# Output rows 12 to 15 of an attention kernel: other order of their products, other place in a step

## The chip, the cores and the metric

The kernel runs on one core of one Trainium2 chip. The metric is the time of one execution on the device in microseconds (us); the median of three runs is 1478.57 us (1478.53 to 1479.0).

## What is computed

Two attention branches over the same input x (2048 positions, width 512, 32 heads of 16) are mixed by a gate. Cut to what matters:

```python
g = sigmoid((x * gate_w).sum(-1, keepdims=True))
# branch A: each position sees itself and 7 earlier ones, 2 apart
a = attention_A(x @ wqkv) @ A_wo
# branch B: full attention, 32 query heads over one head of keys and values
q, k, v = x @ wq, x @ wk, x @ wv
b = softmax(q k^T / 4) v @ B_wo
return g * a + (1 - g) * b
```

All in float32. The kernel multiplies in a reduced format and wins the accuracy back by splitting a factor into a high and a low part, so that one product becomes three: high by high, high by low, low by high.

## The kernel before, in words

Branch B is the long part. It is cut into 32 units (`NU`; 8 groups of heads by 4 blocks of 512 queries) of 16 steps (128 keys each), 512 steps (`NS`) in one loop at the end of the kernel. A step s does, on TensorE (PE):

- the scores, in two pairs of matmuls (`exp_pair`, L487), one pair for each of the banks `eb[0]` and `eb[1]`; ScalarE (ACT) takes the exponential of each pair (L489, 1024 elements a partition) as soon as it stands;
- the weighted sum of the step before, eight matmul instructions into the bank `po` (`weighted`, L497);
- where there are any left, matmuls for the maxima that a later unit will need: a pair into `m2` (`pm` in the profile, L330) between the two pairs of scores, and a single one into `m1` (`ps`) behind them. VectorE (DVE) reduces them (L357, L368). They run ahead of the steps; the last ones, for unit 31, are done in step 480.

At the end of a unit DVE transposes `po` (L511), and some small work on DVE and GpSimd (POOL) makes half a chunk of branch B's output for its 512 positions (`finish_a`, `finish_b`, `finish_c`; then the unit is in `shaped`). Unit 29 is the last one that the last rows wait for before their final chunk: its steps end with step 479.

The output has 16 rows of 128 positions. A row is a sum of products of 512 columns: 12 for branch A (index k = 0: four chunks in three parts, from the tiles `turned`) and, in the last four rows, 9 for branch B (k = 1: three chunks, from the tiles `own`); the fourth chunk comes after the last step. Each product is two matmuls of 64 rows (L848), both halves of the array at once. Rows 12 to 15 are made by the generator `spread`, one product per `yield 0.0`, all into the bank `m2`, which the maxima no longer need then. `spread_some(k)` draws up to k products from it; the loop calls it once a step. What a row needs:

- `blocks_out(j)`, L692: DVE transposes the row of branch A in blocks (L696) into `raw`; `blocks_in` sends that to memory (L701) and back in another order with 16 small DMAs (L707), all on the queue of SyncE (SP);
- `parts_a(j)`, L823: POOL splits it into the two `turned` tiles (two copies L828, two subtractions L831);
- `prepare(j)`, L655: POOL splits branch B's chunks into the two `own` tiles (L660, L665);
- at the end of a row, a copy and an addition on DVE (L867, L868) take the sum out of `m2`; the next row's first product writes `m2` again.

Each of `turned` and `own` has one buffer, so the next row's parts are written when the present row has read the old ones.

The order of instructions on every engine is fixed when the program is built. A small planner keeps a clock per engine (`clk`), gives operations estimated durations (`T_R`, `T_EXP`, ...) and decides by them in which step something is put. `tasks` holds work with a due time, and `run_tasks` at the end of a step issues what is due. The number of products of a step comes from `row_prods` (84 at first): so many are given that 10 (`TO_END`) are left when the steps are over, and at most 4. They run beside the last chain on DVE, from the last weighted sum to the output.

Unit 31's maxima, made in steps up to 480, go back as two extra rows of its queries (`shift_d`, L475): four small DMAs on SP and four on POOL. They must be there when step 496 begins.

Of the kernel before, what the change touches and what calls it, by code (L numbers as in the profile page):

```python
# [19 lines left out]
C = D // P  # L20
# [4 lines left out]
NU = NQB * NHG  # L25
# [12 lines left out]
NS = NU * NJ  # L38
# [3 lines left out]
TO_END = 10  # L42
# [7 lines left out]
def gated_mix_kernel(ctx, tc, xt, wa, wk, wq, wo_a, wo_b, out):  # L50
    nc = tc.nc
# [26 lines left out]
    m2 = pp.tile([P, 2, 512], F32, name="pm")  # L78
# [7 lines left out]
    clk = {"pe": 0.0, "act": 0.0, "dve": 0.0}  # L86
# [221 lines left out]
    half = []  # L308
    free = {"m2": 0.0, "m1": 0.0, "e0": 0.0, "e1": 0.0, "po": 0.0}
    tasks, shifted, pm = [], set(), []  # L310
    hooks, pool, done = [], 0.0, set()
# [20 lines left out]
    def to_go():  # L332
        return 2 * len(slots) + len(half)
# [148 lines left out]
    def exp_pair(s, pr, other=False, first=0):  # L482
        bank, key = (m2, "m2") if other else (eb[pr], f"e{pr}")
        u, kt = divmod(s, NJ)
        for odd in (first, 1 - first):
            b = 64 * odd
            nc.tensor.matmul(bank[:, odd, :], kst[b:b + 64, kt * P:(kt + 1) * P], qst[home(u)[0]][b:b + 64, pr, :], start=True, stop=True)  # L487
        e = px.tile([P, 2, 512], F32, name="pexp", bufs=6)
        nc.scalar.activation(e, bank, AF.Exp, scale=SCALE)  # L489
        free[key] = after("act", after("pe", free[key], T_R) + T_LAT, T_EXP)  # L490
        exped[s] = free[key]
        pexp[s, pr] = e
# [162 lines left out]
    def prepare(j, n, copy=None):  # L655
        nonlocal pool
        hi, lo = turned[j, 1] = [pe[0].tile([P, C, P], F32R, name=f"own{x}", bufs=1) for x in range(2)]
        own = ob[j // 4][:, :n, j % 4 * P:(j % 4 + 1) * P]
        if copy:
            copy(hi[:, :n], own)  # L660
            at = max(clk["pe"], pool / 1e3) + 1.3
        else:
            nc.scalar.activation(hi[:, :n], own, AF.Copy)
            at = after("act", clk["pe"], 0.6)
        nc.gpsimd.tensor_sub(lo[:, :n], own, hi[:, :n].bitcast(F32))  # L665
        pool = max(pool, 1e3 * at) + 1300
# [25 lines left out]
    def blocks_out(j):  # L692

        own = p2[0].tile([P, D], F32, name="raw", bufs=1)
        for k in range(2):
            nc.vector.transpose(own[:, k * D // 2:(k + 1) * D // 2], oa[k][:, j, :])  # L696
        after("dve", 0, 0.9)
        tasks.append((clk["dve"] + 0.3, blocks_in, (j, own)))
# [7 lines left out]
                    dst = oa[k][32 * m:32 * m + 32, j, c * P:(c + 1) * P].rearrange("p (a z) -> p a z", a=4)  # L706
                    nc.sync.dma_start(dst, v[m][:, 2 * k + c])  # L707

    def out_items(j, n):
        items = []  # L710
        for k, m in ((1, n), (0, C)):
            for x, w in ((0, woh), (0, wol), (1, woh)):
                items += [(lambda c=c, x=x, k=k: turned[j, k][x][:, c, :], w[k][:, c, :]) for c in range(m)]
        return items
# [104 lines left out]
    def spread(js, n):  # L819

        m = 3 * (C + n)

        def parts_a(j):  # L823
            nonlocal pool
            hi, lo = turned[j, 0] = [pe[0].tile([P, C, P], F32R, name=f"turned{x}", bufs=1) for x in range(2)]
            for k in range(2):
                own = oa[k][:, j, :].rearrange("p (c q) -> p c q", c=2)
                nc.gpsimd.tensor_copy(hi[:, 2 * k:2 * k + 2], own)  # L828
            for k in range(2):
                own = oa[k][:, j, :].rearrange("p (c q) -> p c q", c=2)  # L830
                nc.gpsimd.tensor_sub(lo[:, 2 * k:2 * k + 2], own, hi[:, 2 * k:2 * k + 2].bitcast(F32))  # L831
            pool = max(pool, 1e3 * clk["pe"]) + 2600

        prepare(js[0], n, nc.gpsimd.tensor_copy)
        yield 1.0
        parts_a(js[0])
        yield 1.0
        while slots or half:
            yield 1.0
        for j in js:  # L840
            nxt = j + 1 if j != js[-1] else None
            items = []
            for i in range(m):
                items = items or out_items(j, n)
                st, mv = items[i]
                for b in range(2):
                    h = slice(64 * b, 64 * b + 64)
                    nc.tensor.matmul(m2[:, b, :], st()[h], mv[h], start=(i == 0), stop=(i == m - 1 and (b == 1 or nxt is not None)))  # L848
                after("pe", 0, T_R)
                row_prods[0] -= 1  # L850
                row_left[0] = m - 1 - i
                if i == 1 and nxt:
                    blocks_out(nxt)
                if i == 3 * n and nxt:
                    prepare(nxt, n, nc.gpsimd.tensor_copy)
                if i < m - 1:
                    yield 0.0
            del turned[j, 0], turned[j, 1]
            x = len(parts)
            if x < 2:  # L860
                spare.append(p2[0].tile([P, 512], F32, name="part", tag=("own", "tr8")[x], bufs=1))
            elif x == 2:
                two = p2[0].tile([P, 2, 512], F32, name="part", tag="pr", bufs=1)
                spare.extend([two[:, 0, :], two[:, 1, :]])
            parts[j] = spare[x]
            if nxt:
                nc.vector.tensor_copy(parts[j], m2[:, 1, :])  # L867
                nc.vector.tensor_add(parts[j], m2[:, 0, :], parts[j])  # L868
                parts_a(nxt)
                after("dve", clk["pe"] + T_LAT, 1.4)  # L870
                yield 1.5
        done.add("last")

    def spread_some(k):

        while (k > 0 or row_left[0] == 1) and later_rows and spread_at[0] <= clk["pe"]:
            x = next(later_rows[0], None)
            if x is None:
                later_rows.clear()
            else:  # L880
                spread_at[0] = clk["pe"] + x
                k -= 1
# [190 lines left out]
    last = len(lumps) - 1  # L1073
# [69 lines left out]
    for s in range(NS + 1):  # L1143
        u, kt = divmod(s, NJ)
        if s == 16 * NB + 4:
            half_back()
        if len(stacked) < NU and s > 16 * (home(len(stacked))[1] + 1):
            stack(len(stacked))
        if s < NS and kt == 0 and u not in shifted:
            while u not in shifted:  # L1150
                clk["pe"] += 0.5
                run_tasks()
                if u not in shifted and left.get(u, 1):
                    assert pause(4)
        v = min(x[0][0] for x in (half, slots, [(NU,)]) if x)
        need = left.get(v, NF // NU)
        steps = 16 * v - 6 - s
        short = need - 2.8 * max(0, steps) if v < NU else 0
        lead = (NF - to_go()) / 64 - s / 16
        order = (0, "m2", "later") if s else ()  # L1160
        rows = 4 if outs else 8
        k, n = (outs + rows) // 4 - 1, C - (outs >= NJ - 4)
        if outs == NJ - 4:
            if s == 16 * NU - 40:
                blocks_out(outs)
            if NU - 3 in shaped and to_go() <= 9 and not later_rows and "last" not in done:
                later_rows.append(spread(list(range(outs, NJ)), n))
            if short > 0 and steps < 2:
                pause(short)
        elif due or outs < NJ and s and kt == 0 and outs // NH in done and NHG * (k + 1) - 1 in shaped and (lead < LEAD or s >= 16 * (NHG * (k + 2) + 1)):  # L1170
            if not due:
                prepare(outs, n)
                due.append(n)
            else:
                out_phase(list(range(outs, outs + rows)), due.pop(), kt == 1)
                outs += rows
                order = (0, "m1", 2)
        elif short > 0 and steps < 2:
            pause(short)

        first = 0
        order = list(order)
        while order:
            which = order.pop(0)
            if which == "later":
                order = ["m1", 1] if free["e1"] > clk["pe"] - E1S else [1, "m1"]
                first = 0
            elif which == "m2":
                fill_ready("m2", M2S)
            elif which == "m1":  # L1190
                if not later_rows and (kt or not s or u >= NU - 8) and singles(s):
                    first = half[0][4] if half else 0
                    fill_ready("m1", M1S)
            elif s < NS:
                exp_pair(s, which % 2 or which // 2, which == 2, first)
        spread_some(min(4, -(-(row_prods[0] - TO_END) // (NS + 1 - s))))
        if s:
            weighted(s - 1)
            if kt == 0 and s < NS:
                finish_a(u - 1, nc.gpsimd)  # L1200
        run_tasks()
        run_pool()
# [63 lines left out]
```

## Time and profile before

| what | value |
|---|---|
| median of three runs | 1478.57 us |
| the profiled execution's own time | 1480.36 us |
| its span in the profile | 1478.3 us |
| PE busy | 1463.2 us, 99% of the span |
| ACT busy | 1274.7 us, 86% |
| DVE busy | 1193.8 us, 81% |
| POOL busy | 1034.4 us, 70% |

The profile is one execution. In it L12 is line 12 of the kernel, `pe`, `pm`, `ps`, `po` are the banks `eb`, `m2`, `m1`, `po`; PEld is the loading of weights, SPq the queue on which SP issues DMAs. A row of the timeline gives start, duration, engine, line, operation, output and inputs, and how many instructions were merged; in brackets stands the idle time before it and who ended that. The chain of waits is the work that ended last, followed back from the end: start, duration, engine, tile, line.

### The profile page before, as it was taken

Reading aid. Unit: us, or ns where it says so; the run is one execution under the profiler, and the core shown is the slowest. Engines: PE = TensorE matmul, PEld = TensorE weight load, DVE = VectorE, ACT = ScalarE, POOL = GpSimd, SP = SyncE. Lnnn points to the kernel's source line nnn. Section 1 sums busy time; section 2 is a strip of 40 time slices with the busy share of each in tenths; the row PEclk is TensorE's granted clock in tenths of the full one; section 3 lists DMA queues with packets and bytes.
Section 4 is the critical chain, followed back from the end, with each engine's and each line's share of the span. In section 5 each row is a group of like instructions: output and inputs, shape, how many; then the busy total and the mean of one; then the engine's idle time right before and its main releaser. Section 6 shows DMA issues by size and latency. Waiting matters only on the chain.

```text
span 1478.3 us, 29547 instructions
## 1 busy us (share of the span) xinstructions
PE 1463.2 (99%) x10996; PEld 708.2 (48%) x10996; DVE 1193.8 (81%) x1855; ACT 1274.7 (86%) x1646; POOL 1034.4 (70%) x1828
## 2 busy tenths in 40 slices
PE   9999999999999999999999999999999999999998
PEld 5998989533333333333333376333333363333343
DVE  6976667789888898888888888889888878888612
ACT  5468988999999999999999978999999988999985
POOL 7876988887988979888889898888888330011221
PEclk9999999999999999999999999999999999999999
DMA  6754323121220211202102011121120000000111
GB/s 223 209 150 136 92 85 122 34 84 42 66 76 10 85 59 41 71 12 70 51 32 81 31 64 67 42 70 42 41 71 12 12 26 16 12 1 2 25 28 36
DMA packets 54080, 89.86 MB, mean 61 GB/s; under 512 B 18800, under 2 KB 35232, under 8 KB 49712
## 3 DMA queue, kind: packets, MB, share of 16 engines
q1 hardware_dynamic: 46928, 48.99, 11.4%
q0 software_dynamic: 6432, 37.94, 7.8%
q8 instruction: 86, 1.41, 0.4%
q10 hardware_dynamic: 576, 1.05, 0.2%
q14 instruction: 58, 0.48, 0.1%
HBM read 60.07 MB, written 27.35 MB: 59 GB/s over the span
## 4 chain that ended last, share of the span: by engine, by line
PE 90%; ACT 3%; POOL 3%; DMA 1%; issue 1%; DVE 1%; DVEq 0%; ACTq 0%; POOLq 0%
PE po L497 34%; PE pe L487 23%; PE pm L330 8%; PE ps L330 7%; PE pe L1094 6%; PE pe L783 4%; PE pm L422 2%; PE ps L422 1%; PE pm L848 1%; POOL qlo L222 1%; ACT dd L432 1%; DMA ad<-stage 1%; POOL qraw L215 1%; PE po L422 1%; PE pe L185 1%
## 5 line engine op out<-in xcount | busy, mean ns | idle before, releaser
L489 ACT ACTIVATE pexp<-pe 128x1024 f32<-128x1024 f32 x1022 | 989.5, 1022 | 95.9 <-PE pe L487 94.1
L357 DVE TENSOR_REDUCE mx<-pm 128x2 f32<-128x1024 f32 x495 | 605.7, 1224 | 118.6 <-PE pm L330 114.8
L497 PE MATMUL po<-pexp,vst 128*32 128x512 f32 x4096 | 545.5, 605 | 0.0
L487 PE MATMUL pe<-qst,kst 64*128 64x512 f32 x1916 | 431.9, 448 | 1.2 <-ACT pexp L489 1.2
L487 PEld LDWEIGHTS pe<-qst,kst 64*128 64x128 f32 x1916 | 179.2, 183 | 476.5 <-ACT pexp L489 470.8
L368 DVE TENSOR_REDUCE mx<-ps 128x1 f32<-128x512 f32 x481 | 327.1, 680 | 3.7 <-PE pe L487 1.9
L330 PE MATMUL pm<-kst,qst 62*128 62x512 f32 x945 | 192.2, 396 | 0.3 <-DVE mx L357 0.3
L561 POOL TENSOR_TENSOR pr<-aext 128x256 f32<-128x256 f32 x256 | 183.1, 742 | 4.3 <-ACT dd L432 4.1
L330 PE MATMUL ps<-kst,qst 62*128 62x512 f32 x455 | 180.1, 396 | 0.2 <-DVE mx L442 0.2
L621 POOL TENSOR_TENSOR oa<-oa,av 128x256 f32<-128x256 f32 x224 | 164.3, 734 | 15.2
L497 PEld LDWEIGHTS po<-pexp,vst 128*32 128x32 f32 x4096 | 80.5, 108 | 178.1 <-issue 169.1
L618 POOL TENSOR_TENSOR av<-aext,lg 128x256 f32<-128x256 f32 x224 | 139.6, 623 | 12.7
L1094 PE MATMUL pe<-wah,xh 64*128 64x384 f32 (+1 forms) x504 | 109.3, 338 | 0.4 <-ACT gate L255 0.4
L1094 PE MATMUL pe<-wal,xh 64*128 64x384 f32 (+1 forms) x504 | 109.7, 338 | 0.0
L1094 PE MATMUL pe<-wah,xl 64*128 64x384 f32 (+1 forms) x504 | 109.5, 337 | 0.0
L432 ACT ACTIVATE dd<-pm 128x512 f32<-128x512 f32 x164 | 90.9, 607 | 17.6 <-PE pm L422 11.9
L442 DVE CUSTOM_DVE_ANT_0 dd<-ps,dd 128x512 f32<-128x512 f32 x82 | 56.7, 692 | 56.7 <-PE ps L422 29.6
L524 POOL TENSOR_TENSOR rl<-rl,gate_t 128x16 f32<-128x16 f32 x31 | 6.9, 222 | 126.2 <-DVE rl L518 125.7
L330 PEld LDWEIGHTS pm<-kst,qst 62*128 62x128 f32 x945 | 91.9, 187 | 2.8 <-DVE mx L357 1.2
L330 PEld LDWEIGHTS ps<-kst,qst 62*128 62x128 f32 x455 | 84.8, 186 | 5.6 <-DVE mx L368 1.7
L567 POOL TENSOR_TENSOR tr<-pr 128x512 f32<-128x512 f32 x64 | 81.8, 1278 | 4.1
L567 POOL TENSOR_TENSOR tr<-tr 128x256 f32<-128x256 f32 (+1 forms) x128 | 72.5, 567 | 8.3
(215 smaller groups left out, 1893.8 us busy)
## 6 DMA issues: line engine op xcount, KB each, us to landing
aext<-ad POOLq DMA_DIRECT2D x32, 1056.0 KB, 5.5
ad<-stage SPq DMA_DIRECT2D x32, 384.0 KB
qst<-qd SPq DMA_DIRECT2D x60, 128.0 KB
xraw<-xt SPq DMA_DIRECT2D x16, 256.0 KB
qd<-qhi SPq DMA_DIRECT2D x16, 256.0 KB
qd<-qlo SPq DMA_DIRECT2D x16, 256.0 KB
qst<-qd SPq DMA_DIRECT2D x60, 64.0 KB
qst<-ml SPq DMA_DIRECT2D x216, 2.0 KB
```

Source lines behind the costliest of these rows:

```text
L330: nc.tensor.matmul(dst, qst[home(v)[0]][b:b + 62, pr, t * P:(t + 1) * P], kst[b:b + 62, kc * 512:(kc + 1) * 512], start=True, stop=True)
L357: nc.vector.tensor_reduce(m[:, :, pr, t, kc], dst, AX.X, ALU.max)
L368: nc.vector.tensor_reduce(m[:, odd, pr, t, kc:kc + 1], dst, AX.X, ALU.max)
L432: nc.scalar.activation(dd[0][:, odd], m2[:, odd, :], AF.Abs)
L487: nc.tensor.matmul(bank[:, odd, :], kst[b:b + 64, kt * P:(kt + 1) * P], qst[home(u)[0]][b:b + 64, pr, :], start=True, stop=True)
L489: nc.scalar.activation(e, bank, AF.Exp, scale=SCALE)
L497: nc.tensor.matmul(po[32 * i:32 * i + 32, :], vst[:, kt, :], pexp[s, i // 2][:, i % 2, :], start=(kt == 0), stop=(kt == NJ - 1))
L561: nc.gpsimd.tensor_mul(pr[:, k], q, e[:, o:o + NH, AC:2 * AC])
L567: nc.gpsimd.tensor_add(nx, cur[:, :, 0:n], cur[:, :, n:2 * n])
L618: nc.gpsimd.tensor_mul(av, e[:, o:o + NH, 2 * AC:].rearrange("p j (h d) -> p j h d", d=DH), lg[:, w].unsqueeze(3).to_broadcast([P, NH, AG, ...
L621: nc.gpsimd.tensor_add(ao, ao, av)
L1094: nc.tensor.matmul(front[2 if x == last else x % 2][0][:, b, :n], l[h], r[h], start=(i == 0), stop=(i == 3 * C - 1))
```

## The change

It does four things to rows 12 to 15:

1. Within a row the 12 products of branch A come first and branch B's 9 after them. So `parts_a` of the next row is issued after the 12th product, and `prepare` of the next row at the row's end; before it was the other way round.
2. The generator is created without waiting for unit 29 to be shaped. It issues `parts_a(12)` first, then waits until no maxima are left and until `m2` is free by the planner's clock. `prepare(12)` is issued as soon as unit 29 is shaped; only the 10th product of row 12 waits for that.
3. `blocks_out` runs a row further ahead: rows 12 and 13 in steps 472 and 480 (before: row 12 in step 472 alone), and the others two rows ahead.
4. The products of a step are given out between its first and its second pair of scores, no longer behind both.

```diff
-    def out_items(j, n):
+    def out_items(j, n, ks=(1, 0)):
         items = []
-        for k, m in ((1, n), (0, C)):
+        for k, m in [(k, n if k else C) for k in ks]:
...
-        prepare(js[0], n, nc.gpsimd.tensor_copy)
-        yield 1.0
         parts_a(js[0])
         yield 1.0
-        while slots or half:
+        while slots or half or free["m2"] > clk["pe"] + 0.1:
             yield 1.0
         for j in js:
             nxt = j + 1 if j != js[-1] else None
             items = []
             for i in range(m):
-                items = items or out_items(j, n)
+                if j == js[0] and i < 3 * C and (j, 1) not in turned:
+                    while i == 3 * C - 3 and NU - 3 not in shaped:
+                        yield 1.0
+                    if NU - 3 in shaped:
+                        prepare(j, n, nc.gpsimd.tensor_copy)
+                items = items or out_items(j, n, (0, 1))
...
-                if i == 1 and nxt:
-                    blocks_out(nxt)
-                if i == 3 * n and nxt:
-                    prepare(nxt, n, nc.gpsimd.tensor_copy)
+                if i == 1 and j + 2 <= js[-1]:
+                    blocks_out(j + 2)
+                if i == 3 * C and nxt:
+                    parts_a(nxt)
                 if i < m - 1:
                     yield 0.0
             del turned[j, 0], turned[j, 1]
+            if nxt:
+                prepare(nxt, n, nc.gpsimd.tensor_copy)
...
                 nc.vector.tensor_add(parts[j], m2[:, 0, :], parts[j])
-                parts_a(nxt)
...
-            if s == 16 * NU - 40:
-                blocks_out(outs)
-            if NU - 3 in shaped and to_go() <= 9 and not later_rows and "last" not in done:
+            if s in (16 * NU - 40, 16 * NU - 32):
+                blocks_out(outs + (s - 16 * NU + 40) // 8)
+            if to_go() <= 9 and not later_rows and "last" not in done:
...
+        some = min(4, -(-(row_prods[0] - TO_END) // (NS + 1 - s)))
...
             elif s < NS:
+                if which == 1:
+                    spread_some(some)
                 exp_pair(s, which % 2 or which // 2, which == 2, first)
-        spread_some(min(4, -(-(row_prods[0] - TO_END) // (NS + 1 - s))))
+        if s == NS:
+            spread_some(some)
```

## The prediction

> **What bounds the kernel now.** I read the page first, then the chain of waits, then the timeline of the last hundred microseconds, engine by engine.
>
> ```profile
> PE 90%; ACT 3%; POOL 3%; DMA 1%; issue 1%; DVE 1%; DVEq 0%; ACTq 0%; POOLq 0%
> ```
>
> PE carries 90% of the chain that ended last. Before step 477 PE is full (scores, maxima and weighted sums), and the change does not touch that part. So only the last 32 steps count. They look like this in the chain of waits:
>
> ```profile
> 1387.50 0.43 PE pe L487 x2
> 1387.93 0.23 PE pm L330 x2
> 1388.17 0.25 PE pe L487 x2
> 1388.41 1.00 PE po L497 x8
> ...
> 1392.07 1.95 ACT pexp L489 x2
> 1394.02 0.04 issue
> 1394.06 0.50 PE pe L487 x2
> ...
> 1406.18 0.66 PE pe L487 x4
> 1406.84 0.70 PE pm L848 x6
> 1407.54 1.00 PE po L497 x8
> ...
> 1465.35 0.42 PE pm L848 x2
> ```
>
> Three kinds of step stand there. While maxima are left, PE does first scores, a pair for the maxima, second scores, weighted sum: 0.43 + 0.23 + 0.25 + 1.00 = 1.91 us of work. When the maxima are over (step 481 on) the chain goes through ACT: the second scores at 1394.06 start only when two exponentials have ended. From 1406 on the chain is PE alone: 0.66 + 0.70 + 1.00 = 2.36 us for a step with three products, so a product costs 0.70 / 3 = 0.23 us and a bare step 2.36 - 0.70 = 1.66 us.
>
> I number the steps back from the last scores, step 511, and measure a step from its first scores on PE to the next step's:
>
> ```profile
> 1393.36 0.49 PE L487 MATMUL pe<-qst,kst 64*128 64x512 f32 x2
> ...
> 1403.52 0.96 PE L487 MATMUL pe<-qst,kst 64*128 64x512 f32 x4
> 1406.11 0.73 PE L487 MATMUL pe<-qst,kst 64*128 64x512 f32 x4
> ...
> 1420.25 0.75 PE L487 MATMUL pe<-qst,kst 64*128 64x512 f32 x4
> 1422.82 0.73 PE L487 MATMUL pe<-qst,kst 64*128 64x512 f32 x4
> 1423.42 1.94 ACT L489 ACTIVATE pexp<-pe 128x1024 f32<-128x1024 f32 x2 [0.63 <-PE pe L487]
> ...
> 1458.18 0.51 PE L487 MATMUL pe<-qst,kst 64*128 64x512 f32 x2
> 1458.91 0.50 PE L487 MATMUL pe<-qst,kst 64*128 64x512 f32 x2 [0.23 <-ACT pexp L489]
> 1460.80 0.74 PE L487 MATMUL pe<-qst,kst 64*128 64x512 f32 x4
> 1462.93 0.96 PE L487 MATMUL pe<-qst,kst 64*128 64x512 f32 x4
> 1463.53 1.94 ACT L489 ACTIVATE pexp<-pe 128x1024 f32<-128x1024 f32 x2 [0.19 <-PE pe L487]
> 1465.70 1.07 PE L497 MATMUL po<-pexp,vst 128*32 128x512 f32 x8
> ```
>
> Step 481 begins at 1393.36, step 486, the first with products, at 1403.52, step 511, the last, at 1462.93. Steps 481 to 485 take 10.16 us, 2.03 each, of which PE works 1.66. That is the empty room. Step 486 takes 1406.11 - 1403.52 = 2.59, step 509 takes 1460.80 - 1458.18 = 2.62, though it holds two products and 510 with two takes 2.13: there the second scores wait for ACT. Step 493, the first of row 13, takes 1422.82 - 1420.25 = 2.57 where 2.36 is usual.
>
> **The change, part by part.**
>
> *When the products start.* The maxima run out in step 480. With at most nine left the generator is made (step 477), POOL splits row 12 of branch A, and the first product falls into step 481: `m2` is free when its last reduction ends, 1392.23 + 1.23 = 1393.46 in the row of DVE further down, and the first product would be ready behind the first scores of 481 at 1393.36 + 0.43 = 1393.79. By the rule for `some`, 74 products in 32 steps, rounded up, give three a step in 481 to 490 and two from 491 on; one row ends on an odd product, so step 506 has three. That is 11 steps of three and 19 of two up to 510, 71 products, and 2, 1 and 10 after, as before. Before it was three in 486 to 506 and two after.
>
> Steps 481 to 485 then take 5 x 2.36 = 11.80 instead of 10.16, and 15 products leave later steps, 15 x 0.23 = 3.45: a gain of about 1.8 us (1.5 to 1.9 with a product at 0.22 to 0.235).
>
> *Where they stand in a step.* PE's sum is the same in either order, 2.36 with three and 2.13 with two: the steps of 1387.50, with a pair between the scores, show that something in the middle costs its own 0.23 and no more. What goes is PE's wait for ACT. In the new order, counted from first scores at 0 with two products: first exponential at 0.60 (1462.93 to 1463.53), two of them end at 0.60 + 1.94 = 2.54; the next step's second scores come at 2.13 + 0.43 + 0.46 = 3.02. In the old order they would come at 2.13 + 0.66 - 0.25 = 2.54, the very moment, so that any lateness of ACT holds PE. With the products ahead of them there is room of half a microsecond. So the stalls of step 486 (2.59 - 2.36 = 0.23) and 509 (2.62 - 2.13 = 0.49) go: 0.7 us. The second began with a late exponential that the profile does not explain; bounds 0.2 to 0.72. ACT does not become the bound: with three products the second scores start at 0.43 + 0.70 = 1.13 and stand 0.50 later at the latest, 1.6, when the first exponential ends (0.60 + 0.97). What is late next is PE itself.
>
> Adding up directly, from step 481 to 511: 11 x 2.36 + 19 x 2.13 = 66.43, and three row ends at 0.22, 67.1; before 1462.93 - 1393.36 = 69.57. The gain is 2.5, as by the two terms.
>
> *The end.* The last weighted sum starts 1465.70 - 1462.93 = 2.77 after the scores of step 511. New order: 0.43 + 0.46 + 0.25 + 1.00 + 0.42 = 2.56 on PE, but the last exponential ends at 2.54 and needs a moment to be seen: 2.6. Gain 0.15 (0 to 0.2). Behind it nothing changes: ten products beside the same chain on DVE.
>
> *What is moved on the other queues.*
>
> ```profile
> 1392.23 1.23 DVE L357 TENSOR_REDUCE mx<-pm 128x2 f32<-128x1024 f32 x1 [0.89 <-PE pm L330]
> ...
> 1396.42 0.73 DVE L696 STREAM_TRANSPOSE raw<-oa 128x256 f32<-128x256 f32 x2
> ```
>
> DVE: row 13's two transpositions (0.73) are now issued in step 480, ahead of the last maxima; they fit into the 0.89 that DVE idles before 1392.23, so they cost nothing; without that room the last reduction, and `m2`, would be later by up to 0.7. Row 14's come at about 1394.5 and push the work that shapes unit 29 back by 0.8.
>
> ```profile
> 1396.61 2.58 SPq L475 DMA_DIRECT2D qst<-ml  x4
> 1399.29 0.35 SPq L701 DMA_DIRECT2D td<-raw  x1
> 1401.33 7.98 SPq L707 DMA_DIRECT2D oa<-td  x16
> ```
>
> SP: a row is one DMA out, about two until the first back (1399.29 to 1401.33), then 16 in 8, so 10 us. Rows 13 and 14 now stand on SP from 1392.2 to 1412.4, and the four DMAs of unit 31's maxima, before at 1396.61, behind both, since the planner issues them a step later: 1412.4 to 1415.0. Step 496 needs them at 1393.36 + 10 x 2.36 + 5 x 2.13 + 0.22 = 1427.8. They are covered by 10 us or more of steps.
>
> ```profile
> 1399.81 1.00 POOL L665 TENSOR_TENSOR own<-ob,own 128x384 fp32r<-128x384 f32 x1
> ```
>
> POOL: `prepare(12)` ended at 1400.81 (L665 at 1399.81); 0.8 later is 1401.6, and the first product that reads it is in step 485, at 1393.36 + 4 x 2.36 + 0.43 = 1403.2. `parts_a(13)` needs row 13 back by SP (1402.3 and some two more to land), ends by about 1407 and is read at 1410. At a row's end `prepare` has 12 products of time, and `parts_a` 9, three steps, for four instructions smaller than this one. I count all of this as nothing; the tightest cover is the 1.6 us of step 485.
>
> *Row ends.*
>
> ```profile
> 1420.10 0.69 DVE L868 TENSOR_TENSOR part<-pm,part 128x512 f32<-128x512 f32 x1
> ```
>
> The copy and this addition end at 1420.79, and the next product, due behind the scores of 1420.25, comes late: the step is 2.57, so 0.21 lost, three times. Between the last product of a row and the first of the next stand the same instructions on PE in both orders (second scores, weighted sum, first scores, 1.66 us). So I keep 0.22 x 3 in both; the bounds are no change and all 0.65 gained. The waiting product now holds back second scores too. ACT idles 0.63 before the step that follows such an end (1423.42), which covers it.
>
> The Trainium skill, "TensorE: Matmul & The Clock Gate", section "Step-by-step: what each phase is for", says that matmuls stay in program order and only weight loads are pulled ahead. This speaks against the change, since a product that waits for `m2` now stops scores and exponentials behind it; by that rule a row end could cost up to its 0.2 three times more, 0.6, and the sum would be 2.0. In this trace the queue behaves in order (the scores of 1458.91 hold what follows), but ACT's room takes it.
>
> Sum: 1.8 + 0.7 + 0.15 + 0 = 2.6 us. The profiled execution took 1480.36, span 1478.3 and 2.06 around it; it would be about 1477.8 with a span of 1475.7. The median lies 1.8 below that execution, so I forecast 1478.57 - 2.6 = **1475.95**. What a measurement here can tell from no change is about 0.2%, 2.96 us: the forecast lies just inside.
>
> **The rivals.**
>
> *Row ends are hidden too.*
>
> ```profile
> L848 PEldq EVENT_SEMAPHORE  x3: 51/51/51, 1420.8 to 1454.3; - x3
> ```
>
> At the three row ends PE's queue has a separate semaphore instruction (51 ns, first at 1420.8). If that or the 0.1 us that DVE is late goes in the new order, 0.4 to 0.65 more is gained, 3.0 to 3.3 in all: 1475.3. For it: the lack is small. Against: the same PE work lies between.
>
> *The change does less than it says.* If unit 29 is shaped later than I count, or POOL's split of it, the tenth or 13th product of row 12 waits. Behind a waiting product stand scores now, so each us of that wait is a us of PE; 1 to 2 us are lost and 0.6 to 1.6 gained: 1477.4. For it: the cover is 1.6 us, out of steps worked out by hand.
>
> *SP's queue becomes the bound.* The 32 small DMAs for rows 13 and 14 stand ahead of unit 31's maxima. If they take longer than the 8 us a row, being issued on end, row 13 is late for step 488 and, from 13 us more in all, step 496 waits. At 16 instead of 8 a row the maxima land at about 1433, 5 us late, and row 13's split ends near 1415, 5 late: both together cost 5 to 9, less 2.6 gained, so 1478.57 + 4.4 = 1483.0. For it: SP waits in order for each row's way out. Against: the 7.98 us for 16 leave 10 us of cover. The Trainium skill, "DMA: Bandwidth & Descriptors", section "Anatomy of one DMA — SWDGE (gpsimd) path", says that waits happen on the issuing sequencer before dispatch; the trace agrees, with two us of SP between 1399.29 and 1401.33.
>
> **How the numbers follow.** The forecast, 1475.5 to 1476.5 with its bounds (stalls 0.2 to 0.7, product cost): 62%. Row ends hidden: 20%, 1475.0 to 1475.6. Less than it says: 11%, 1476.5 to 1478.0. SP's queue: 7%. The range from 1475.1 to 1477.3 takes in the forecast, most of the second and half of the third. Faster by over 0.2% (under 1475.61): 20% and the forecast's own lower edge, 4%, so 24%. Slower: 7%. The rest, 69%, within 0.2%.
>
> **What would show it.** Right: products from about 1393.7 on; steps of 2.36 and then 2.13 without gaps on PE; ACT no longer in the chain after 1392; first scores of step 511 about 2.5 earlier, the last weighted sum 2.6. Wrong: steps of 2.2 and more with two products (the middle costs), second scores waiting for ACT, a product of row 12 waiting for POOL, step 488 or 496 waiting for a DMA. The forecast falls if row ends cost nothing, or cost more because scores stand behind them.

## The result, and the profile after

The changed kernel takes 1475.39 us (1475.33 to 1475.84, 13 runs) against 1478.59 before (1478.4 to 1479.24, 13 runs): 3.20 us less, a ratio of 0.9978 with a 95% interval of 0.9969 to 0.9986. The forecast was 1475.95 in a range of 1475.1 to 1477.3. The profiled execution took 1475.43, its span is 1473.6.

The chain of waits of the kernel after, for the steps 481, 488 and 511 (L848 is now L851):

```profile
1391.77 0.43 PE pe L487 x2
1392.20 0.72 PE pm L851 x6
1392.92 0.23 PE pe L487 x2
1393.15 0.99 PE po L497 x8
...
1408.30 0.44 PE pe L487 x2
1408.74 0.90 PE pm L851 x6
1409.64 0.23 PE pe L487 x2
1409.87 1.00 PE po L497 x8
...
1458.61 0.43 PE pe L487 x2
1459.04 0.46 PE pm L851 x4
1459.50 0.23 PE pe L487 x2
1459.73 0.99 PE po L497 x8
1460.72 0.43 PE pm L851 x2
```

From step 481 to the last weighted sum ACT has left the chain: first scores, products, second scores, weighted sum follow one another on PE without a gap, 0.43 + 0.72 + 0.23 + 0.99 = 2.37 us. The exception is a step that begins a row (1408.74): its three products take 0.90 instead of 0.69.

The timeline of the same kernel, with the rows that answer to the steps' starts, and to what DVE, POOL and SP were to do:

```profile
1389.59 0.76 DVE L696 STREAM_TRANSPOSE raw<-oa 128x256 f32<-128x256 f32 x2
...
1390.57 1.23 DVE L357 TENSOR_REDUCE mx<-pm 128x2 f32<-128x1024 f32 x1 [0.23 <-PE pm L330]
...
1391.69 0.50 PE L487 MATMUL pe<-qst,kst 64*128 64x512 f32 x2
...
1398.67 1.01 POOL L665 TENSOR_TENSOR own<-ob,own 128x384 fp32r<-128x384 f32 x1
...
1401.50 0.86 PE L851 MATMUL pm<-woh,own 64*128 64x512 f32 x6
...
1408.23 0.51 PE L487 MATMUL pe<-qst,kst 64*128 64x512 f32 x2
...
1409.71 2.59 SPq L475 DMA_DIRECT2D qst<-ml  x4
...
1410.79 0.50 PE L487 MATMUL pe<-qst,kst 64*128 64x512 f32 x2
...
1430.53 0.51 PE L487 MATMUL pe<-qst,kst 64*128 64x512 f32 x2
...
1447.45 0.50 PE L487 MATMUL pe<-qst,kst 64*128 64x512 f32 x2
...
1458.54 0.50 PE L487 MATMUL pe<-qst,kst 64*128 64x512 f32 x2
...
1461.13 1.06 PE L497 MATMUL po<-pexp,vst 128*32 128x512 f32 x8
```

Step 481 starts at 1391.69, 1.67 earlier than in the trace of before; that much the two executions differ ahead of the change, so only stretches are compared. Steps 481 to 511: 1458.54 - 1391.69 = 66.85 us against 69.57. Scores of step 511 to last weighted sum: 2.59 against 2.77. Together 2.72 + 0.18 = 2.90 of the 3.20 us. From the last weighted sum to the end of the span it is 1473.6 - 1461.13 = 12.47 against 1478.3 - 1465.70 = 12.60, but these 0.13 are not the change's: up to the start of DVE's last additions it is 5.81 in both, and what follows, these additions and the result's way to memory, takes 6.58 to 6.85 in the ten traces, without regard to the version.

Most of the rest lies outside the span. An execution's time is longer than its span: by 1.84 us in the changed kernel (median of the 13 executions; 1.78 to 1.90), by 2.12 in the kernel before (median of the 54 executions beside the experiments; 2.06 to 2.17). The two do not overlap, so 0.28 of the 3.20 us is gained where no row of a profile shows anything. The kernel with part 4 alone (further down) has 2.11, the ones with parts 1 to 3 have 1.75 to 1.84: these 0.28 come with the first three parts. Their cause stays open.

Eight steps of two products, 498 to 505, take (1447.45 - 1430.53) / 8 = 2.115 us. The first step of row 13 takes 1410.79 - 1408.23 = 2.56.

### The profile page after: what moved, and what is told of

Read it like the earlier page. It is cut to its first block, busy times and chain, and to the rows that moved or that the text cites. A ratio compares the mean times of both kernels' runs of the same rounds, so it can differ in the third digit from the quotient of the medians.

```text
span 1473.6 us, 29548 instructions
## 1 busy us (share of the span) xinstructions
PE 1461.7 (99%) x10996; PEld 708.0 (48%) x10996; DVE 1193.9 (81%) x1855; ACT 1274.5 (86%) x1646; POOL 1032.6 (70%) x1828
## 4 chain that ended last, share of the span: by engine, by line
PE 91%; ACT 3%; POOL 3%; issue 1%; DVE 1%; DMA 1%; DVEq 0%; POOLq 0%; ACTq 0%
PE po L497 35%; PE pe L487 23%; PE pm L330 8%; PE ps L330 7%; PE pe L1098 7%; PE pe L783 4%; PE pm L422 2%; PE ps L422 1%; PE pm L851 1%; ACT dd L432 1%; PE po L422 1%; POOL qlo L222 1%; POOL qraw L215 1%; PE pe L185 1%; DMA xraw<-xt 1%
```

## The experiments

The first four ran on one chip, the last four on another; the kernel before took 1479.34 us beside the first four and 1479.11 beside the last four. So differences to the kernel before are compared, not times. The 95% interval of a ratio reaches about 0.0009 to each side, 1.3 us: by it the first three experiments cannot be told from the kernel before. What they show rests on stretches of their traces, one execution each, and on the medians of their spans. In the expectations the times stand against 1478.59.

**The products behind both scores again.** All else of the change stays.

```diff
-                if which == 1:
-                    spread_some(some)
                 exp_pair(s, which % 2 or which // 2, which == 2, first)
-        if s == NS:
-            spread_some(some)
+        spread_some(some)
```

> The changed kernel with one part undone: the products of a step stand behind both pairs of scores again; start, order and row-ahead stay. Theory (the place removes PE's waits for ACT in the second scores): with three products a step nothing waits, but with two the second scores come at 2.12 + 0.34 after a step's start and their bank is free at about 2.58, so about every second of 19 such steps loses 0.13, 1.2 us together; step 508's late exponential costs 0.3 again and the end 0.17: 1475.4 + 1.7 = 1477.1. Rival (the place does nothing, the early start is the whole gain): 1475.4, and steps with two products keep 2.12.

Measured: 1479.03, 0.3 below the kernel before, ratio 1.0001 (0.9992 to 1.0009; the medians alone give 0.9998). The medians of the spans are the same, 1477.2, so the 0.3 lies outside the span. The whole gain of the steps is gone, 2.9 us and not the theory's 1.7. The traced execution is the longest of the eleven, 1482.75, but its surplus lies ahead of step 481: from there to the end of the span it is 84.80 us, before 84.94. The timeline of PE and ACT shows where the gain went:

```profile
1396.10 0.49 PE L487 MATMUL pe<-qst,kst 64*128 64x512 f32 x2
1396.82 0.50 PE L487 MATMUL pe<-qst,kst 64*128 64x512 f32 x2 [0.23 <-ACT pexp L489]
...
1420.37 0.74 PE L487 MATMUL pe<-qst,kst 64*128 64x512 f32 x4
...
1420.97 1.94 ACT L489 ACTIVATE pexp<-pe 128x1024 f32<-128x1024 f32 x2 [0.41 <-PE pe L487]
...
1422.49 0.96 PE L487 MATMUL pe<-qst,kst 64*128 64x512 f32 x4
...
1424.85 0.74 PE L487 MATMUL pe<-qst,kst 64*128 64x512 f32 x4
...
1426.98 0.97 PE L487 MATMUL pe<-qst,kst 64*128 64x512 f32 x4
...
1429.34 0.73 PE L487 MATMUL pe<-qst,kst 64*128 64x512 f32 x4
...
1465.71 0.96 PE L487 MATMUL pe<-qst,kst 64*128 64x512 f32 x4
```

The steps of two alternate: 2.12, 2.36, 2.13, 2.36. In every second one the four matmuls of the scores take 0.96 instead of 0.74, because the second pair waits for ACT: in the step of 1422.49 the loading of its weights waits for ACT until 1422.96, just behind the two exponentials of 1420.97, which end at 1422.91. The pattern is the one that was expected, the price of a wait is 0.23 and not 0.13, and step 481 itself waits too (2.84). From step 481 to 511 it is 1465.71 - 1396.10 = 69.61 us, as before the change (69.57): the early start without the new place is worth nothing in the steps.

**The place alone**, in the kernel before; start in step 486, branch B first.

```diff
             elif s < NS:
+                if which == 1:
+                    spread_some(some)
                 exp_pair(s, which % 2 or which // 2, which == 2, first)
-        spread_some(min(4, -(-(row_prods[0] - TO_END) // (NS + 1 - s))))
+        if s == NS:
+            spread_some(some)
```

> The kernel before with one part done alone: the products stand between first and second scores, but start in step 486 and keep branch B first. Theory: the stalls of steps 486 and 509 and 0.15 at the end go, 0.85 to 1.3 us: 1477.3 to 1477.7; steps 481 to 485 keep 2.03. Rival (the place does nothing): 1478.6. Second rival (the place carries most): under 1476.5.

Measured: 1478.55, 0.79 below the kernel before, ratio 0.9995 (0.9986 to 1.0004). Its trace:

```profile
1392.42 0.50 PE L487 MATMUL pe<-qst,kst 64*128 64x512 f32 x2
...
1402.59 0.50 PE L487 MATMUL pe<-qst,kst 64*128 64x512 f32 x2
...
1461.30 0.50 PE L487 MATMUL pe<-qst,kst 64*128 64x512 f32 x2
...
1463.89 1.06 PE L497 MATMUL po<-pexp,vst 128*32 128x512 f32 x8
```

Steps 481 to 485 take 1402.59 - 1392.42 = 10.17 us, as before; the stretch to step 511 takes 68.88, 0.69 less, and 2.59 to the last weighted sum, 0.18 less. That is the theory's 0.85, and the medians of the spans agree (1476.4 against 1477.2).

**The first product held until step 486**, in the changed kernel.

```diff
-        while slots or half or free["m2"] > clk["pe"] + 0.1:
+        while slots or half or at_step[0] < 486 or free["m2"] > clk["pe"] + 0.1:
             yield 1.0
```

> The changed kernel, its first product held until step 486 as before; all else of the change stays. Theory: five steps lose 2.03 - 1.66 = 0.37 each of filled room, 1.85 us: 1477.2; and within 0.2 of the kernel before with the place alone, since then the order of the branches is worth nothing. Rival (the start is worth nothing, as PE's sum is the same): 1475.4. Rival (branch A first matters by itself): this one lies over 0.4 from the kernel with the place alone.

Measured: 1477.97, 1.37 below the kernel before, ratio 0.9992 (0.9983 to 1.0001).

```profile
1392.63 0.49 PE L487 MATMUL pe<-qst,kst 64*128 64x512 f32 x2
...
1402.80 0.51 PE L487 MATMUL pe<-qst,kst 64*128 64x512 f32 x2
...
1461.55 0.50 PE L487 MATMUL pe<-qst,kst 64*128 64x512 f32 x2
...
1464.14 1.06 PE L497 MATMUL po<-pexp,vst 128*32 128x512 f32 x8
```

In the trace it is the kernel with the place alone: 68.92 to step 511 against 68.88, and to the end of the span 1476.6 - 1392.63 = 83.97 against 1476.4 - 1392.42 = 83.98. So in the steps the order of the branches and the rows fetched ahead are worth nothing by themselves; they only let the products start. By the times alone the rival's mark, over 0.4 apart, is met: the medians lie 0.58 apart. But 0.36 of it is outside the span (1.75 against 2.11), and the medians of the spans lie 0.2 apart, 1476.2 and 1476.4. Against the changed kernel's 66.85 holding the products back costs 2.07 in the trace and 1.8 in the time, where the theory said 1.85.

**A third bank**, so that a row's first product need not wait for the addition.

```diff
+            banks = (m1 if j in (js[0], js[2]) else m2[:, 0, :], m2[:, 1, :])
...
-                    nc.tensor.matmul(m2[:, b, :], st()[h], mv[h], ...)
+                    nc.tensor.matmul(banks[b], st()[h], mv[h], ...)
...
-                nc.vector.tensor_copy(parts[j], m2[:, 1, :])
-                nc.vector.tensor_add(parts[j], m2[:, 0, :], parts[j])
+                nc.vector.tensor_copy(parts[j], banks[1])
+                nc.vector.tensor_add(parts[j], banks[0], parts[j])
```

> The changed kernel, with the upper half of the products of rows 12 and 14 going into the bank m1, which the maxima have left, so that a row's first product waits only for the copy of the row before, not for the addition behind it. Theory (a row end loses 0.2 because the first product waits for the addition on DVE): three row ends fall from 2.34 and 2.56 to 2.12 and 2.36, 0.65 us in all: 1474.75. Rival (the loss is the separate semaphore instruction or a restart of the matmul stream): row ends keep at least half of it, 1475.1 to 1475.4.

Measured: 1475.6, 3.74 below the kernel before, ratio 0.9975 (0.9965 to 0.9984); 0.54 more than the 3.20 of the changed kernel, where the theory said 0.65. Its timeline:

```profile
1408.64 0.51 PE L487 MATMUL pe<-qst,kst 64*128 64x512 f32 x2
...
1411.00 0.51 PE L487 MATMUL pe<-qst,kst 64*128 64x512 f32 x2
...
1428.02 0.69 DVE L874 TENSOR_TENSOR part<-pm,part 128x512 f32<-128x512 f32 x1
...
1428.41 0.49 PE L487 MATMUL pe<-qst,kst 64*128 64x512 f32 x2
...
1428.74 0.40 PE L852 MATMUL ps<-woh,turned 64*128 64x512 f32 x1
...
1428.77 0.50 PE L852 MATMUL pm<-woh,turned 64*128 64x512 f32 x1
...
1430.66 0.50 PE L487 MATMUL pe<-qst,kst 64*128 64x512 f32 x2
...
1449.94 0.51 PE L487 MATMUL pe<-qst,kst 64*128 64x512 f32 x2
...
1452.07 0.50 PE L487 MATMUL pe<-qst,kst 64*128 64x512 f32 x2
```

Two row ends are down to a plain step (2.36 and 2.13), the middle one to 2.25. So the loss at a row end goes with the wait for the addition, as the theory has it; the separate semaphore instruction is not its cause, for there are still three. A restart of PE's stream that comes only with such a wait is not told apart from it: in the changed kernel the first product of row 13 starts 0.1 late and the step loses 0.20. The middle end keeps 0.13. There the previous row's addition still reads `m2` (`pm`) and ends at 1428.71, and the first product's lower half, which goes into `m2`, starts right behind it, at 1428.77; in the other two ends the addition reads `m1`. So that half probably still waits for the addition. This was not tested.

**The changed kernel again**, beside the next three.

> The changed kernel as it is, beside the next three on one chip and for a second trace of it. Expected: 3.0 to 3.3 us under the kernel before, steps 481 to 511 again 66.8 to 66.9 us, row ends again 0.2 each.

Measured: 1475.92, 3.19 below the kernel before, ratio 0.9979 (0.997 to 0.9987), 66.83 us from step 481 to 511.

**More products for the end.**

```diff
-TO_END = 10
+TO_END = 12
```

> The changed kernel with 12 products kept for the time after the last step and not 10. Theory (PE alone is the bound from step 481 on, and after the last weighted sum DVE's chain is): two steps lose a product, 0.46 us, and the stretch from the last weighted sum to the end stays 12.4 to 12.5: 0.45 under the changed kernel. Rival (PE is bound in that stretch too): the stretch grows by 0.46, no gain.

Measured: 1475.45, 0.47 below the changed kernel beside it, though some runs of the two overlap; ratio to the kernel before 0.9975 (0.9965 to 0.9985). In the trace steps 481 to 511 take 66.30, 0.53 less than the 66.83. The last weighted sum and what hangs on it:

```profile
1460.62 1.06 PE L497 MATMUL po<-pexp,vst 128*32 128x512 f32 x8
...
1463.82 0.86 PE L851 MATMUL pm<-woh,own 64*128 64x512 f32 x6
...
1466.44 1.88 DVE L1243 TENSOR_TENSOR osl<-pe,part 128x512 f32<-128x512 f32 x3
```

The stretch from the last weighted sum to the end is 1473.1 - 1460.62 = 12.48 us, as with ten products (12.47). There was room on PE beside DVE's chain for two more.

**Both together**, with 12 and with 13 products for the end.

> The third bank and 12 products kept for the end together. The third bank has shown 0.47 us from step 481 to 511. Theory (both are plain time of PE and add): 0.9 to 1.0 us under the changed kernel.

> The third bank and 13 products kept for the end. Theory: another 0.23 from the steps, but PE's last products now end behind the first part of DVE's result, so the stretch after the last weighted sum grows by 0 to 0.25: 0.9 to 1.2 us under the changed kernel.

Measured: 1475.04 and 1474.98, 0.88 and 0.94 below the changed kernel; ratios to the kernel before 0.9973 (0.9962 to 0.9983) and 0.9972 (0.9962 to 0.9983). The two gains add up. The 13th product brings nothing that can be told. It is taken from step 511, and there the last weighted sum waits for ACT instead, as this kernel's timeline shows:

```profile
1460.87 1.06 PE L497 MATMUL po<-pexp,vst 128*32 128x512 f32 x8 [0.18 <-ACT pexp L489]
...
1466.79 1.89 DVE L1244 TENSOR_TENSOR osl<-pe,part 128x512 f32<-128x512 f32 x3
```

From the last weighted sum to DVE's additions it is 5.92 us, with 12 products alone 5.82 (1460.62 to 1466.44). All runs of these two versions lie below all runs of the changed kernel beside them (at most 1475.42 against at least 1475.62).

## Why the prediction was right, and where its steps were not

- **When the products start.** Right: step 481, three a step to 490 and in 506, two otherwise.
- **A step's length.** Three products: 2.36, right. Two: 2.115, not 2.13, which was read from a single step of the old order (510). Over 19 steps that is 0.3 us. So the third product of a step is worth 2.36 - 2.115 = 0.245 and not 0.23. The bounds given for the early start, 1.5 to 1.9, do not follow from a product at 0.22 to 0.235; with 11.80 us for the five steps they would be 1.7 to 1.9.
- **How far the forecast fell short.** It gave 2.6 and the change brought 3.2. About 0.25 of the difference is the stretch of the steps (66.85 measured, 67.1 forecast), 0.03 the end, and 0.28 lies outside the span, which the prediction took to be the same before and after ("2.06 around it"). That the time fell within the range is no credit to this last part: no step of the working looked there.
- **The two terms.** Here the reasoning has a gap, though its sums held. "A gain of about 1.8 us" for the early start was worked out as if it did not matter where in a step the products stand. It holds only with the new place: with it the early start brings 2.07 in the trace and 1.8 in the time, without it nothing in the steps. The place without the early start brings 0.87 in the trace, where 0.7 and 0.15 were forecast. So the two terms add up, but only in this order, the place first. The prediction had seen that in steps of two the second scores come "the very moment" their bank is free, but counted only the two stalls that the trace of before happens to hold. Before, most steps with products had three; the early start makes 19 of them steps of two, and in the old place about every second one waits 0.2. The place is what makes the room usable.
- **The end.** Right: 2.59 against 2.6 forecast, 0.18 gained.
- **The other queues.** Right. DVE's two transpositions fit into its gap (idle 0.23 left before 1390.57). `prepare(12)` ended at 1399.68 and was read at 1401.50, a cover of 1.8 where 1.6 was counted. Unit 31's DMAs left SP by 1412.3, 13.8 us ahead of step 496 (1426.08).
- **Row ends.** Right: 0.20 to 0.23 lost at each of the three, as before. The third bank shows that the loss goes with the wait for the addition. The second scores stand behind the late product (1408.74, then 1409.64). The rule of the Trainium skill ("TensorE: Matmul & The Clock Gate", section "Step-by-step: what each phase is for"), that matmuls stay in program order, agrees with this. The further 0.6 us that the order could have cost did not come: ACT still has room, since after such an end it waits for PE before the next exponentials, here 0.47 us in the changed kernel:

```profile
1411.39 1.94 ACT L489 ACTIVATE pexp<-pe 128x1024 f32<-128x1024 f32 x2 [0.47 <-PE pe L487]
```

- **The rivals.** The measured time lies in the band of the first rival (1475.0 to 1475.6), nearer to its 1475.3 than to the forecast, but not by its mechanism: the row ends kept their loss. The other two did not come about.

## What to carry to other kernels

When work is to fill another engine's slack, look at where in the in-order queue it is put. Here, behind the matmuls that waited for ACT, the products filled nothing; ahead of them they cost only their own 0.23 to 0.25 us each, and the wait was gone. Price each part of a change with the others and without them: the early start was worth 2 us with the new place and nothing without it. To see this beforehand, build the period of a step in both orders, for every number of items that a step will have, and not only for those that the trace holds. And compare spans as well as times: a part of a difference can lie outside the span, where no row explains it.

## What the runs showed that was not expected

Step 508 has a late exponential in every kernel, wherever its products stand. In the changed kernel:

```profile
1452.13 0.51 PE L487 MATMUL pe<-qst,kst 64*128 64x512 f32 x2
...
1453.02 1.94 ACT L489 ACTIVATE pexp<-pe 128x1024 f32<-128x1024 f32 x2 [0.67 <-PE pe L487]
```

It starts 0.89 us after its scores, where 0.60 is usual; in all ten traces it is 0.87 to 0.89 (before: 1456.04 to 1456.92). In the old place this cost PE 0.49 in step 509, in the new one 0.06 (2.18 instead of 2.12). Its cause stays open.
